# Spectral mixing and a top-80 expert layer: the kept rows chosen from short lists made during the forward part

## The chip, the cores and the metric

The kernel runs on one core of a Trainium2 chip. The metric is the device time of one execution in microseconds. The kernel before takes 773.69 us (median of three runs, 771.19 to 774.16). Every time below comes from one profiled execution of the kernel before.

## The reference

Two steps in fp32. First a spectral filter over each of 8 sequences of 2496 rows of 256 numbers:

```python
X = np.fft.rfft(x, axis=1)               # x: (8, 2496, 256)
Y = X * (filt_r + 1j * filt_i)[None]     # 1249 frequencies x 256
y = np.fft.irfft(Y, n=2496, axis=1)      # (8, 2496, 256) -> 19968 rows
```

Then an expert layer on the 19968 rows of `y`. A row belongs to the one expert of 8 with its largest logit; of each expert's rows the 80 with the largest gate weight are kept, all other rows of the output are zero:

```python
logits = x @ w_gate                      # (19968, 8)
expert_idx = np.argmax(logits, axis=1)
gate_w = softmax(logits)[arange, expert_idx]
for e in range(8):
    tok_idx = rows of expert e, cut to the 80 largest gate_w
    h = np.maximum(x[tok_idx] @ w1[e], 0.0)               # 256 -> 1024
    out[tok_idx] = gate_w[tok_idx, None] * (h @ w2[e])    # 1024 -> 256
```

So only 640 of the 19968 rows of `y` are needed as rows; of the others only the logits are.

## The kernel before

A sequence is a grid of 39 x 64 rows, and its transform is two sets of matmuls with a turn between them.

*Start (L155 to L171, L204 to L215, L173 to L181).* `load_tables` puts the tables and the two filters (four pieces of up to 0.66 MB, `fst`) on the DMA queue of ScalarE (ACT). `load_x` brings a sequence's rows in chunks on SyncE's queue (SP). `stage1` multiplies a chunk by `wf_t`, ACT copies the result out of PSUM and stores it to the scratch `d1` in DRAM. `turn_filter` transposes the filters on TensorE.

*Forward part (`manual_schedule`, the loop over sequences at its end).* Here the written order is the order of each engine. For sequence `b` there are twelve steps `u`: `stage2` (matmuls with `d_t`, products with the filter on VectorE, two additions on GpSimd), `stage1` of the sequence after, two steps later `turn`, which stores the spectrum to the scratch `yf[b]` on GpSimd's queue, and `load_t2` for the next sequence. The gate logits of a pair of sequences are worked out from their spectra, in five parts (`logits`), inside the sequences after the pair, and land in `lg`: 128 partitions x 256 rows x 8 experts. The logits of the last pair follow the loop.

*Selection (`select`, L532 to L858).* It starts when all of `lg` is there. Softmax and argmax give each row a key per expert (its gate weight under its own expert, else zero); keys are transposed to 128 partitions of 1248. The 80th largest key of each expert is searched for in 9 rounds of 7 counting passes over all keys (L667), with a small matmul behind each round. Then positions are worked out by running sums, and one-hot matmuls turn them into lists (L766 to L781): `idxb` (up to 128 kept rows of each sequence), and for each of the 80 places of an expert `idxs` (output row), `idxg` (place in `y_sel`) and `gate`. `more` counts rows beyond 128 of a sequence.

*Zero stores and weights.* `zero_t` is stored 32 times over `out`, 0.64 MB each, on the SP queue, and the weights of the first five experts are loaded on that queue (two transfers of 1.05 MB for an expert).

*Back transform (`back`).* For each sequence: an indirect DMA on GpSimd's queue gathers 128 rows (10 KB each) of a table of inverse-transform rows by `idxb`, SP loads the spectrum `yb` (2.62 MB), TensorE makes 20 transposes of the gathered rows and 20 matmuls with `yb`, and the 128 rows go to the scratch `y_sel`. `gt`, `yb` and the rest have two buffers each. If `more` is above zero, further lists of rows follow, else the branch is skipped. At the branch the SP queue waits until its transfers have landed.

*Expert stage (`gather`, `layer1`, `layer2`).* Per expert: gather 80 rows of `y_sel` by `idxg`, two layers of matmuls, scatter to `out` by `idxs`.

Outside `manual_schedule` the framework chooses the order of the instructions of each engine from their dependences; a tile pool that opens where another has closed waits for the last use of the memory under it.

## Time and profile before

| | us |
|---|---|
| median of three runs | 773.69 |
| the profiled execution, its own time | 774.0 |
| its span in the trace | 772.2 |
| PE busy | 482.4 (62%) |
| VectorE (DVE) busy | 362.8 (47%) |
| GpSimd (POOL) busy | 226.8 (29%) |
| ScalarE (ACT) busy | 123.4 (16%) |

Busy time is summed over the whole span, and stages with different limits lie in it: a share says little until the span is cut into stages. PE is TensorE's matmuls, PEld its weight loads, which run beside them. The transfers of the whole span are 162.15 MB, 210 GB/s on the mean. The granted clock (PEclk) is TensorE's, as a fraction of full speed, 1.00 being 2.4 GHz and 0.50 being 1.2 GHz. The DMA share is the mean busy share of the core's 16 DMA engines.

### The profile page before, as it was taken

To read this page: it belongs to the slowest core of one execution; us is meant where nothing else is said; L and a number is where in the kernel's file an instruction comes from. 1 tells how busy PE (TensorE), PEld (TensorE's weight loads), DVE (VectorE), ACT (ScalarE), POOL (GpSimd) and SP (SyncE) were. 2 spreads that over 40 slices of the span, in tenths; PEclk is the share of its full clock that TensorE was granted. 3 is DMA by queue.
4 is the path that set the end of the run, shared out by engine and by line. 5 is a ranking of instruction groups with operands and counts; after the bars stand their busy time and mean duration, and the time that the engine had idled before them with its cause. 6 is when DMAs were issued, how large, how long until landed. Compare 5 with 4: busy or idle time off the path is not lost. (4 is left out here: it accounts for less than half of the span.)

```text
span 772.2 us, 8200 instructions
## 1 busy us (share of the span) xinstructions
PE 482.4 (62%) x3004; PEld 387.4 (50%) x3004; DVE 362.8 (47%) x519; ACT 123.4 (16%) x210; POOL 226.8 (29%) x302
## 2 busy tenths in 40 slices
PE   3258797998899979892100000122431999987996
PEld 1146666775777768780100000102431888877885
DVE  1033343253435434637798999899980221210110
ACT  0213342333333424220000000000000100100111
POOL 1003645354636555763510000001931000002111
PEclk9567998999999999985555555555555999995999
DMA  9999999799989997999992000000007789812720
GB/s 175 234 285 219 295 314 304 225 276 310 301 267 293 314 304 251 297 415 408 366 382 71 0 0 0 0 0 1 0 1 312 274 334 374 346 50 76 235 73 14
DMA packets 63573, 162.15 MB, mean 210 GB/s; under 512 B 6519, under 2 KB 38263, under 8 KB 61159
## 3 DMA queue, kind: packets, MB, share of 16 engines
q1 hardware_dynamic: 47222, 101.84, 41.0%
q10 hardware_dynamic: 8624, 26.94, 11.8%
q0 software_dynamic: 7680, 32.77, 11.5%
q8 instruction: 26, 0.43, 0.2%
q14 instruction: 21, 0.16, 0.1%
HBM read 96.26 MB, written 65.27 MB: 209 GB/s over the span
## 5 line engine op out<-in xcount | busy, mean ns | idle before, releaser
L241 DVE TENSOR_TENSOR p<-pb,ft 128x512 f32<-128x512 f32 x160 | 102.7, 686 | 156.0 <-issue 91.6
L212 PE MATMUL pa<-x,wf_t 117*120 117x512 f32 x176 | 94.5, 663 | 30.4 <-ACT t L214 17.5
L246 POOL TENSOR_TENSOR yt<-p,p 128x256 f32<-128x256 f32 x80 | 57.9, 724 | 170.5 <-DVE p L241 170.2
L234 PE MATMUL pb<-d_t,t 128*128 128x128 f32 x640 | 88.2, 283 | 22.1 <-DMA t<-d 22.1
L667 DVE TENSOR_SCALAR_CACHE_REDUCE junk<-keyT,thr 128x1248 bf16<-128x1248 f32 x63 | 95.3, 1512 | 6.5 <-ACT keyT L636 4.2
L234 PEld LDWEIGHTS pb<-d_t,t 128*128 128x128 f32 x640 | 81.8, 198 | 32.6 <-issue 32.5
L258 PEld LDWEIGHTS py<-gi,yt 128*128 128x128 f32 x640 | 82.9, 192 | 28.3 <-issue 14.2
L258 PE MATMUL py<-gi,yt 128*128 128x136 f32 x640 | 90.1, 284 | 10.6 <-POOL yt L248 9.9
L768 POOL TENSOR_TENSOR vals<-vv,oh_bf 128x1536 bf16<-128x1536 bf16 x8 | 34.8, 4382 | 148.5 <-PE psl L780 148.4
L403 PE MATMUL pr<-yb,wt 128*128 128x256 f32 x320 | 71.7, 379 | 0.0
L672 PE MATMUL pc<-cnt,grp 128*128 128x7 f32 x18 | 5.3, 365 | 105.1 <-DVE junk L667 105.1
L214 ACT COPY t<-pa 120x512 f32<-120x512 f32 x88 | 51.3, 586 | 114.2 <-PE pa L212 104.7
L403 PEld LDWEIGHTS pr<-yb,wt 128*128 128x128 f32 x320 | 59.6, 190 | 7.4
L266 ACT COPY ysp<-py 128x544 f32<-128x544 f32 x80 | 48.9, 612 | 87.8 <-PE py L258 82.2
L212 PEld LDWEIGHTS pa<-x,wf_t 117*120 117x120 f32 x176 | 32.0, 202 | 59.0 <-issue 39.4
L248 POOL TENSOR_TENSOR yt<-p,p 128x256 f32<-128x256 f32 x80 | 57.8, 722 | 0.0
L672 PEld LDWEIGHTS pc<-cnt,grp 128*128 128x128 f32 x18 | 4.5, 312 | 106.1 <-DVE junk L667 70.6
L400 ACT COPY wt<-pw 128x512 f32<-128x512 f32 x16 | 9.4, 587 | 291.8 <-PE pw L398 291.8
L780 PE MATMUL psl<-vals,ohp 128*80 128x48 bf16 x256 | 18.6, 242 | 38.2 <-DVE ohp L775 38.2
L780 PEld LDWEIGHTS <-ohp 128*80 128x80 bf16 x256 | 17.7, 181 | 40.6 <-DVE ohp L775 40.6
L775 DVE TENSOR_TENSOR ohp<-pos,iota_bf 128x2560 bf16<-128x2560 bf16 x8 | 37.4, 4738 | 0.0
L464 PEld LDWEIGHTS ph<-xs,w 128*128 128x128 f32 x256 | 36.1, 227 | 0.6
(161 smaller groups left out, 482.6 us busy)
## 6 DMA issues: line engine op xcount, KB each, us to landing
t<-d SPq DMA_DIRECT2D x80, 256.0 KB
yf<-ysp POOLq DMA_DIRECT2D x40, 512.0 KB, 7.5
yb<-yf SPq DMA_DIRECT2D x8, 2560.0 KB
out_dram<-zero_t SPq DMA_DIRECT2D x32, 624.0 KB
d<-t ACTq DMA_DIRECT2D x40, 480.0 KB
x<-in_x_dram SPq DMA_DIRECT2D x120, 156.0 KB
w<-in_moe_w_dram SPq DMA_DIRECT2D x16, 1024.0 KB
d<-t ACTq DMA_DIRECT2D x8, 240.0 KB
```

The costliest lines, as they stand in the source:

```text
L212: nc.tensor.matmul(out=ps[0:NM1], lhsT=wf_t, rhs=xt[:, 2 * i:2 * i + 2, :], start=True, stop=True)
L214: nc.scalar.copy(out=t1[:, 2 * i:2 * i + 2, :], in_=ps[0:NM1])
L234: nc.tensor.matmul(out=ps[:, i, cb], rhs=d_t[:, s, :], start=True, stop=True, lhsT=st["t2", b, s // SG][:, s % SG, 128 * cb:128 * cb + 128])
L241: nc.vector.tensor_tensor(out=pt, in0=ps[:].rearrange("p s c r q -> p (s c) r q"), in1=f.unsqueeze(2).to_broadcast([128, 2 * NDB, 2, NQ]), ...
L246: nc.gpsimd.tensor_tensor(out=yt[:, :, 0, :], in0=pr[0][:, :, 0, :], in1=pr[1][:, :, 1, :], op=AL.subtract)
L248: nc.gpsimd.tensor_tensor(out=yt[:, :, 1, :], in0=pr[0][:, :, 1, :], in1=pr[1][:, :, 0, :], op=AL.add)
L258: nc.tensor.matmul(out=ps[:, i, 136 * cb:136 * cb + 136], rhs=gi[:, cb, :], lhsT=yt[:, 2 * i + cb].rearrange("p r q -> p (r q)"), start=Tr ...
L266: nc.scalar.copy(out=ys[:, m:m + 2, :], in_=ps[:, :, 0:ZW])
L403: nc.tensor.matmul(po[:], lhsT=wt[:, s, :], rhs=yb[:, s, :], start=(start and s == 0), stop=(stop and s == NS - 1))
L667: nc.vector.tensor_scalar(out=junk[:], in0=keys, scalar1=thr[:, j:j + 1], scalar2=None, op0=AL.is_ge, op1=AL.add, accum_out=cnt[:, j:j + 1],)
L775: nc.vector.tensor_tensor(out=ohp[:], in0=pos[:, t0:t0 + TC].unsqueeze(2).to_broadcast([PG, TC, cap]), in1=iota_bf[:].unsqueeze(1).to_broa ...
L780: nc.tensor.matmul(psl[0:cap, :], lhsT=ohp[:, t, :], rhs=vals[:, t, :, :], start=(t0 + t == 0), stop=(t0 + t == T - 1))
```

## The change

*Gating in the forward part.* When a pair's logits are done, `gating` works in six parts: softmax and argmax of this pair alone, the gates stored to a scratch `gates_dram` (four stores on GpSimd's queue), keys transposed on TensorE, and VectorE's `max` and `max_index` on each sequence. A transposed partition is 8 experts x 16 groups of rows, so for each sequence there are 128 *cells* of 156 keys, and the 8 largest of each cell with their places go to `cand` and `code`. Pairs 0 to 2 are gated in sequences 3, 5 and 7 (steps 1, 2, 4, 5, 7, 9), the last pair behind the loop.

*`pick` in place of `select`.* Of each partition's 64 candidates the 16 largest are taken, brought to one partition per expert by a matmul (256 numbers), and ten times `max`, nine times `match_replace` give the 80 largest and so the edge. Counts, positions and the lists come from small matmuls and one-hot products on the kept candidates. `gate` is gathered from `gates_dram` by eight indirect DMAs (`gather_gates`).

*Fallback.* `bad` is above zero if a cell's eighth candidate is kept, a partition keeps 16 or more, a sequence keeps more than 128 rows, or an expert's count isn't 80. Only then do the old `select`, the back transform and the spill lists run, inside one `If`.

*Start.* Filters come in ten pieces through the buffers of `t2` on GpSimd's queue, as do `d_t`, `gi`, `e_t` and `wi_t`.

*SP queue.* Two spectra are asked for ahead of `pick`; the zero stores and the weights are spread over the rounds of the back transform.

The diff, cut (the constants, most of `pick` and the one-hot lists are left out; a line that is only "..." marks each cut):

```diff
-                for k, filt in enumerate((filt_r, filt_i)):
-                    for q in range(2):
-                        off, step = (0, C) if q == 0 else (N1 * C, -C)
-                        nc.scalar.dma_start(
-                            out=fst[k][32 * q:32 * q + 32],
-                            in_=bass.AP(tensor=filt.tensor, offset=filt.offset + off,
-                                        ap=[[N1 * C, 32], [step, NS], [1, C]]))
-                nc.scalar.dma_start(out=d_t, in_=d_dram.ap())
...
+                nc.gpsimd.dma_start(out=d_t, in_=d_dram.ap())
...
+        def load_filter(k, g):
+            fst[k, g] = t2pool.tile([128, SG, C], F32, name=f"fst_{k}_{g}", tag="t2")
+            filt = (filt_r, filt_i)[k]
+            for q in range(2):
+                off, step = (0, C) if q == 0 else (N1 * C, -C)
+                nc.gpsimd.dma_start(
+                    out=fst[k, g][32 * q:32 * q + 32],
+                    in_=bass.AP(tensor=filt.tensor, offset=filt.offset + off + step * SG * g,
+                                ap=[[N1 * C, 32], [step, SG], [1, C]]))
...
+        def gating(b2, part):
+            T2 = 2 * NJ
+            l = lg[:, T2 * b2:T2 * b2 + T2, :]
...
+            if part == 0:
+                mx = row("mx")
+                nc.vector.tensor_reduce(out=mx[:], in_=l, axis=AX.X, op=AL.max)
+                st["sh"] = big("sh")
+                nc.vector.tensor_tensor(out=st["sh"][:], in0=l, in1=bc(mx[:]), op=AL.subtract)
+                st["ex"] = big("ex")
+                nc.scalar.activation(out=st["ex"][:], in_=st["sh"][:], func=AF.Exp)
+            elif part == 1:
+                st["first"] = big("first")
+                nc.vector.scalar_tensor_tensor(
+                    out=st["first"][:], in0=st["sh"][:], scalar=0.0,
+                    in1=rev[:].unsqueeze(1).to_broadcast([128, T2, E]),
+                    op0=AL.is_equal, op1=AL.mult)
+                st["fm"] = row("fm")
+                nc.vector.tensor_reduce(out=st["fm"][:], in_=st["first"][:], axis=AX.X,
+                                        op=AL.max)
+            elif part == 2:
+                gw = row("gw")
+                nc.vector.tensor_reduce(out=gw[:], in_=st["ex"][:], axis=AX.X, op=AL.add)
+                nc.vector.tensor_scalar(out=gw[:], in0=gw[:], scalar1=1e-9, scalar2=None,
+                                        op0=AL.add)
+                st["gw"] = row("gwr")
+                nc.vector.reciprocal(out=st["gw"][:], in_=gw[:])
+            elif part == 3:
+                oh = big("oh")
+                nc.vector.tensor_tensor(out=oh[:], in0=st["first"][:], in1=bc(st["fm"][:]),
+                                        op=AL.is_equal)
+                st["key"] = big("key")
+                nc.vector.tensor_tensor(out=st["key"][:], in0=oh[:], in1=bc(st["gw"][:]),
+                                        op=AL.mult)
+                for h in range(2):
+                    for i in range(2):
+                        g0 = (2 * b2 + i) * S + NJ * h
+                        nc.gpsimd.dma_start(
+                            out=bass.AP(tensor=gates_dram.tensor, offset=gates_dram.offset + g0,
+                                        ap=[[N2, N1], [1, NJ]]),
+                            in_=st["gw"][64 * h:64 * h + N1, NJ * i:NJ * i + NJ])
+            elif part == 4:
+                pk = fps.tile([128, 4, 2, 64], F32, name=f"pk_{b2}", tag="f")
+                for i in range(4):
+                    nc.tensor.transpose(pk[:, i].rearrange("p h n -> p (h n)"),
+                                        st["key"][:, 16 * i:16 * i + 16, :], ident[:])
+                st["kt"] = gpool.tile([128, 2, N1, 2, 2], F32, name=f"kt_{b2}", tag="kt")
+                for i in range(2):
+                    nc.scalar.copy(out=st["kt"][:, i].rearrange("p n h c -> p c h n"),
+                                   in_=pk[:, 2 * i:2 * i + 2, :, 0:N1])
+            else:
+                for i in range(2):
+                    b = 2 * b2 + i
+                    k = st["kt"][:, i].rearrange("p n h c -> p (n h c)")
+                    nc.vector.max(out=cand[:, b, :], in_=k)
+                    nc.vector.max_index(out=cidx[:, b, :], in_max=cand[:, b, :], in_values=k)
+                nc.vector.scalar_tensor_tensor(
+                    out=code[:, 2 * b2:2 * b2 + 2, :], in0=cidx[:, 2 * b2:2 * b2 + 2, :],
+                    scalar=16.0, in1=cbase[:, 2 * b2:2 * b2 + 2, :], op0=AL.mult, op1=AL.add)
...
+            for k, g in kg[:7]:
+                load_filter(k, g)
             load_tables(1)
...
+                    if b % 2 == 1 and b > 1 and u in (1, 2, 4, 5, 7, 9):
+                        gating(b // 2 - 1, (1, 2, 4, 5, 7, 9).index(u))
...
+            for part in range(NG):
+                gating(B // 2 - 1, part)
...
-    for i in range(4 * B):
-        nc.sync.dma_start(
-            out=out[i * ZR:i * ZR + ZR, :].rearrange("r d -> (r d)").rearrange(
-                "(p m) -> p m", p=128),
-            in_=zero_t[:])
-    for e in range(3):
-        load_weights(e)
+    zeros = list(range(4 * B))
+    def put_zeros(n):
+        for i in zeros[:n]:
+            nc.sync.dma_start(
+                out=out[i * ZR:i * ZR + ZR, :].rearrange("r d -> (r d)").rearrange(
+                    "(p m) -> p m", p=128),
+                in_=zero_t[:])
+        del zeros[:n]
...
+        for i in range(NTOP):
+            src = pall if i == 0 else left
+            nc.vector.max(out=top[:, 8 * i:8 * i + 8], in_=src[:])
+            if i + 1 < NTOP:
+                nc.vector.match_replace(out=left[:], in_to_replace=top[:, 8 * i:8 * i + 8],
+                                        in_values=src[:], imm_value=-1.0)
...
+        viol = sp.tile([128, 4], F32, name="viol")
+        nc.vector.tensor_reduce(out=viol[:, 0:1], in_=kept[:, :, KC - 1], axis=AX.X, op=AL.add)
+        nc.vector.tensor_scalar(out=viol[:, 1:2], in0=rcnt[:], scalar1=float(KR), scalar2=None,
+                                op0=AL.is_ge)
+        vb = sp.tile([128, B], F32, name="vb")
+        nc.vector.tensor_scalar(out=vb[:], in0=poff[:, 1, 0:B], scalar1=128.0, scalar2=None,
+                                op0=AL.is_gt, op1=AL.add, accum_out=viol[:, 2:3])
+        vt = sp.tile([128, 1], F32, name="vt")
+        nc.vector.tensor_scalar(out=vt[:], in0=tau[:], scalar1=1e-20, scalar2=None, op0=AL.is_gt)
+        nc.vector.scalar_tensor_tensor(
+            out=viol[:, 3:4], in0=poff[:, 2, 1:2], scalar=float(cap), in1=vt[:],
+            op0=AL.not_equal, op1=AL.mult)
...
+    def gather_gates():
+        nc.gpsimd.memset(gate[:], 0.0)
+        for e in range(E):
+            nc.gpsimd.indirect_dma_start(
+                out=gate[:, e:e + 1], out_offset=None, in_=gates_dram[:, :],
+                in_offset=bass.IndirectOffsetOnAxis(ap=idxs[:, e:e + 1], axis=0),
+                bounds_check=N - 1, oob_is_err=False)
...
+        yb = {b: spectrum(mp, b, f"{b}") for b in range(2)}
+        put_zeros(8)
+        with (
+            tc.tile_pool(name="pick", bufs=1) as sp,
+            tc.tile_pool(name="pkps", bufs=1, space=PSUM) as pp,
+        ):
+            pick(sp, pp)
         for b in range(B):
-            back(mp, mps, f"{b}", lambda: spectrum(mp, b, f"{b}"), 128 * b, idxb[:, b:b + 1])
...
+            back(mp, mps, f"{b}", lambda: yb.pop(b), 128 * b, idxb[:, b:b + 1])
+            if b + 2 < B:
+                yb[b + 2] = spectrum(mp, b + 2, f"{b + 2}")
+            put_zeros(3)
+            if b >= 3:
+                load_weights(b - 3)
+            if b == 2:
+                gather_gates()
...
+    n_bad = nc.values_load(bad[0:1, 0:1], min_val=0, max_val=1 << 20)
+    with tc.If(n_bad > 0):
+        select(tc, lg, cap, ident, ident_bf, iota, iota_i, pid, pid_i, lane, idxs, idxg, gate,
+               idxb, more, nof, ohb)
+        with (
+            tc.tile_pool(name="xp2", bufs=1) as mp,
+            tc.tile_pool(name="xps2", bufs=1, space=PSUM) as mps,
+        ):
+            for b in range(B):
+                back(mp, mps, f"g{b}", lambda: spectrum(mp, b, f"g{b}"), 128 * b,
+                     idxb[:, b:b + 1])
+            for t in range(NX):
+                ix = spill_lists(tc, mp, mps, t, cap, nof, ohb, iota, idxg)
+                po = None
+                for b in range(B):
+                    po = back(mp, mps, f"x{t}_{b}", lambda: spectrum(mp, b, f"x{t}_{b}"),
+                              128 * (B + t) if b == B - 1 else None, ix[:, b:b + 1],
+                              start=(b == 0), stop=(b == B - 1), acc=po, pad=True)
...
-    for e in range(3, 5):
-        load_weights(e)
```

On SP, between the last loads of the forward part and the spectrum of round 3 of the back transform. `w_0` to `w_4` are experts' weights, `yb` spectra, `y_sel` the rows made by a round (`yr`) or the zeros behind them. Before (the 32 zero stores and `w_0` to the first half of `w_2` stand ahead of this):

```order
L358 DMA w_2_2775<-in_moe_w_dram 128x8x256
L425 DMA y_sel<-zero_t 128x256 x4
L356 DMA w_3_6100<-in_moe_w_dram 128x2x1024
L358 DMA w_3_6102<-in_moe_w_dram 128x8x256
L356 DMA w_4_6104<-in_moe_w_dram 128x2x1024
L358 DMA w_4_6106<-in_moe_w_dram 128x8x256
L426 TENSOR_LOAD more
L426 ISA x2
L413 DMA yb_3491<-yf_81 128x5120
L413 DMA yb_3550<-yf_82 128x5120
```

and after:

```order
L496 DMA out_dram<-zero_t 128x1248 x10
L713 DMA yb_2954<-yf_119 128x5120
L713 DMA yb_2956<-yf_120 128x5120
L496 DMA out_dram<-zero_t 128x1248 x10
L488 DMA w_0_3387<-in_moe_w_dram 128x2x1024
L708 DMA y_sel<-yr_3168 128x256
L713 DMA yb_3171<-yf_121 128x5120
L490 DMA w_0_3389<-in_moe_w_dram 128x8x256
L708 DMA y_sel<-yr_3230 128x256
L713 DMA yb_3233<-yf_122 128x5120
L496 DMA out_dram<-zero_t 128x1248
```

The spectra have moved ahead of 22 zero stores and all weights, and a spectrum no longer has only spectra and small stores around it. The memory under `yb_2954` and `yb_2956` is that of the last gating, so they, and all that stands behind them, wait for its end.

On SP, at the end of the back transform. Before:

```order
L413 DMA yb_3904<-yf_88 128x5120
L408 DMA y_sel<-yr_3840 128x256
L408 DMA y_sel<-yr_3899 128x256
L408 DMA y_sel<-yr_3958 128x256
L427 COMPARE_AND_BRANCH
```

and after:

```order
L496 DMA out_dram<-zero_t 128x1248 x3
L488 DMA w_3_3583<-in_moe_w_dram 128x2x1024
L490 DMA w_3_3585<-in_moe_w_dram 128x8x256
L708 DMA y_sel<-yr_3641 128x256
L496 DMA out_dram<-zero_t 128x1248 x3
L488 DMA w_4_3647<-in_moe_w_dram 128x2x1024
L490 DMA w_4_3649<-in_moe_w_dram 128x8x256
L738 DMA y_sel<-zero_t 128x256 x4
L739 TENSOR_LOAD bad
L739 ISA x2
L740 COMPARE_AND_BRANCH
```

Before, three small stores stand in front of the branch at which the queue waits for its transfers; after, the last rounds' zero stores and weights stand there too.

On ACT, at the start of the program. `fst` are the filters, `t` the results of `stage1`, `d` the scratch. Before:

```order
L155 DMA wf_t<-wf_tbl 117x120
L160 DMA fst_131<-in_filt_r_dram 32x5120
L160 DMA fst_131<-in_filt_r_dram 32x20x256
L160 DMA fst_132<-in_filt_i_dram 32x5120
L160 DMA fst_132<-in_filt_i_dram 32x20x256
L164 DMA d_t<-d_tbl 128x2560
L165 DMA gi<-in_moe_w_gate_dram 128x8
L166 DMA gi<-in_moe_w_gate_dram 128x8
L214 ACT_TABLE_LOAD
L214 COPY t_0_0_166<-pa_0_0_167 120x512
```

and after:

```order
L205 DMA wf_t<-wf_tbl 117x120
L267 ACT_TABLE_LOAD
L267 COPY t_0_0_219<-pa_0_0_220 120x512
L267 COPY t_0_0_219<-pa_0_1_223 120x512
L268 DMA d_0_218<-t_0_0_219 120x1024
```

The seven transfers that stood ahead of ACT's first copy are gone from its queue.

## Rows read from the trace of the kernel before

**Rows 1.** Stages: from:to, length, busy (instructions) PE PEld DVE ACT POOL, PEclk, DMA share, GB/s.

```profile
0.00:59.90 59.90, 22.65 (x103) 12.60 (x103) 8.88 (x14) 7.53 (x12) 3.44 (x12) 0.71 0.95 231
59.90:320.00 260.10, 235.51 (x1487) 184.43 (x1488) 105.28 (x160) 89.17 (x150) 132.69 (x211) 0.96 0.93 282
320.00:339.30 19.30, 17.17 (x144) 16.45 (x143) 11.64 (x19) 4.90 (x8) 17.66 (x28) 1.00 1.04 387
339.30:355.20 15.90, 12.39 (x63) 7.70 (x62) 4.87 (x6) 1.55 (x3) 2.97 (x9) 0.60 1.02 413
355.20:598.60 243.40, 37.66 (x332) 31.71 (x333) 205.56 (x274) 3.59 (x5) 49.68 (x21) 0.50 0.29 109
598.60:692.90 94.30, 91.00 (x480) 78.03 (x480) 19.99 (x32) 9.39 (x16) 5.63 (x6) 0.98 0.72 280
...
697.00:772.20 75.20, 66.02 (x400) 56.45 (x400) 6.53 (x16) 7.27 (x16) 14.66 (x16) 0.84 0.31 102
```

**Rows 2.** Groups: line, engine, operation, out<-in, count | busy, mean ns | idle before.

```profile
L667 DVE TENSOR_SCALAR_CACHE_REDUCE junk<-keyT,thr 128x1248 bf16<-128x1248 f32 x63 | 95.3, 1512 | 6.5 <-ACT keyT L636 4.2
...
L273 POOL DMA_DIRECT2D yf<-ysp x40 | 31.0, 776 | 0.0
...
L605 DVE TENSOR_REDUCE mx<-lg 128x256 f32<-128x2048 f32 x1 | 2.3, 2275 | 0.0
...
L840 DVE TENSOR_TENSOR ohl<-plcf,iota 80x1024 f32<-80x1024 f32 x1 | 1.2, 1221 | 0.0
L351 POOL MEMSET zero_t<- 128x1248 f32 x1 | 1.1, 1138 | 2.4 <-PE pa L212 2.4
...
L683 DVE TENSOR_SCALAR tau<-base 128x1 f32<-128x1 f32 x1 | 0.2, 155 | 0.0
```

**Rows 3.** Timeline from 353 us: start, duration, engine, line, operation [idle before <-releaser].

```profile
353.04 2.17 DVE L308 COPY lg<-pl 39x512 f32<-39x512 f32 x2 [3.75 <-PE pl L303]
...
355.38 2.91 DVE L566 TENSOR_SCALAR n_i<-pid_i 128x1 int32<-128x1 int32 x1
...
356.19 2.02 POOL L690 MEMSET wT<- 128x2048 bf16 x1
```

**Rows 4.** Timeline, end of the selection and first round of the back transform.

```profile
582.44 0.17 DVE L847 CAST idxb<-plist 128x8 int32<-128x8 f32 x1 [3.68 <-PE plist L845]
582.54 1.24 SPq L413 DMA_DIRECT2D yb<-yf  x2
583.51 1.07 POOL L389 DMA_INDIRECT gt<-rows_tbl,idxb  x1 [16.95 <-DVE idxb L847]
...
598.62 1.73 PE L398 MATMUL pw<-ident,gt 128*128 128x128 f32 x7 [16.21 <-DMA gt<-rows_tbl,idxb]
...
611.43 0.32 SPq L413 DMA_DIRECT2D yb<-yf  x1
```

**Rows 5.** The tile `gt` (gathered table rows), time from issue to landing.

```profile
DMA to landing us min/median/max: 6.6/10.2/19.8
```

**Rows 6.** Timeline, end of the back transform.

```profile
692.42 0.42 DVE L407 COPY yr<-pr 128x256 f32<-128x256 f32 x1 [7.51 <-PE pr L403]
...
696.97 0.94 POOL L447 DMA_INDIRECT xg<-y_sel,idxg  x1 [34.74 <-DVEq L427]
```

**Rows 7.** Two stretches in which the DMA engines are full, columns as in Rows 1.

```profile
340.00:403.00 63.00, 15.90 (x75) 10.77 (x74) 47.07 (x69) 4.65 (x8) 21.29 (x21) 0.52 1.03 388
583.00:599.00 16.00, 0.38 (x2) 0.41 (x3) 0.00 (x0) 0.00 (x0) 2.04 (x2) 0.50 0.98 392
```

**Rows 8.** Timeline of the start.

```profile
12.26 11.23 ACTq L160 DMA_DIRECT2D fst<-in_filt_i_dram  x2
...
32.91 1.07 ACT L214 COPY t<-pa 120x512 f32<-120x512 f32 x2
33.55 8.86 PE L212 MATMUL pa<-x,wf_t 117*120 117x512 f32 x14 [17.46 <-ACT t L214]
...
59.86 2.05 PE L234 MATMUL pb<-d_t,t 128*128 128x128 f32 x8 [9.35 <-DMA t<-d]
```

More of the change, by code (lines that the diff above doesn't have):

```diff
@@ new lines @@
+    same = consts.tile([128, 128], BF16, name="same")
+    nc.vector.tensor_scalar(out=same[:], in0=ecol[:], scalar1=lane[:, 0:1], scalar2=None,
+                            op0=AL.is_equal)
+    before = consts.tile([128, 128], BF16, name="before")
+    nc.vector.tensor_scalar(out=before[:], in0=iota[:], scalar1=pid[:, 0:1], scalar2=None,
+                            op0=AL.is_gt)
+    before_e = consts.tile([128, 128], BF16, name="before_e")
+    nc.vector.tensor_tensor(out=before_e[:], in0=before[:], in1=same[:], op=AL.mult)
@@ L124 @@
+    ones_bf = consts.tile([128, 128], BF16, name="ones_bf")
+    nc.gpsimd.memset(ones_bf[:], 1.0)
     yf = [dpool.tile([128, NS, C], F32, name=f"yf_{b}") for b in range(B)]
@@ L150 @@
         ft = [tpool.tile([128, NS, NDB, NQ], F32, name=f"ft{i}") for i in range(2)]
-        fst = [stg.tile([NQ, NS, C], F32, name=f"fst{i}") for i in range(2)]
+        fst = {}
         def load_tables(part):
@@ L317 @@
                 load_x(0, ch)
+            kg = [(k, g) for k in range(2) for g in range(NS // SG)]
+            for k, g in kg[:7]:
+                load_filter(k, g)
             load_tables(1)
```

213 lines of the change are left out of this document (183 added, 30 removed).

## Prediction

> **What bounds the kernel now.** I read the busy table by stage first. In [rows 1] the reader is to see seven stretches of one execution (span 772.2 us; its own time 774.0 us, the median of the three runs 773.69, so the sum below is made against 774.0 and needs no correction). From 59.9 to 320 us TensorE is busy 235.5 of 260.1 us: the forward part is a TensorE stage with transfers close behind (DMA share 0.93). From 320 to 339.3 it is GpSimd that is full, 17.66 of 19.3 us. From 355.2 to 598.6 us, 243.4 us, TensorE does 37.7 us of work, the DMA share is 0.29, and VectorE is busy 205.6 us: this is the selection, and the granted clock is 0.50 in it. From 598.6 to 692.9 TensorE is full again (91.0 of 94.3 us), in the per-sequence back transform. The expert stage takes the last 75.2 us.
>
> The groups by line name the work of the selection: 63 counting passes of 1512 ns (95.3 us) lead [rows 2]. The timeline gives its ends. The logits of the last pair of sequences are copied by VectorE until 355.2 us [rows 3]; the row lists `idxb` are written at 582.44 us; the first gather is issued 1 us later and lands when TensorE starts, 598.6 us [rows 4]. At the end of the back transform, 4.1 us lie between the last copy at 692.9 and the gather that opens the expert stage [rows 6].
>
> **The change part by part.** For the price of a small VectorE instruction I take a line through [rows 2, 6]: 256 elements 0.42 us, 1024 elements 1.22, 2048 elements 2.28, so about 0.15 us plus 1.04 ns per element.
>
> *Selection, removed: 243.4 us* [rows 1], from the last logits to TensorE's first transpose. In its place stand three pieces in a row.
> (a) Gating of the last pair. Seven passes over 512 elements at 0.68 us (4.8), reciprocal and offset (0.7, the reciprocal has no row of that size), four transposes with two copies behind them (about 2), the list instructions (about 1.2) and the hops between engines: 10 us. The other three pairs are gated inside the forward part.
> (b) `pick`. Nineteen instructions of MAX and MATCH_REPLACE over 256 elements have no row in this trace. The nearest is a pass of 256 elements at 0.42 us [rows 6]; the bounds are 0.15 us (a one-element instruction) and 1.51 us (the slowest list-like pass here, the counting pass) [rows 2]. At 0.42 they cost 8.0 us, and lie between 2.9 and 28.7. The rest: two one-hot passes of 1024 elements (2.4), one of 1280 (1.5), four passes of 128 to 256 (1.3), six list instructions of 64 elements (1.3), some 24 tiny ones at 0.16 (3.8), three or four trips over TensorE at about 0.75 and the small matmuls (4). Together 22 us, bounds 17 and 43.
> (c) The first gather. Its eight kind landed after 6.6 to 19.8 us, median 10.2 [rows 5]. The first of before took 15.1 us because two 2.6 MB spectra were issued in the same microsecond [rows 4]; now those were issued 22 us earlier, and zero stores share the engines. I take 10.2.
> Sum: 10 + 22 + 10.2 = 42.2 us for 243.4, that is -201.2.
>
> *What the selection covered.* In the long stretch the SP queue put out most of the 32 zero stores and five experts' weights, for nothing. That cover is gone. The order of the SP queue now has ten zero stores, then the first two spectra, which wait for the end of the last gating (the memory under them is its lists), ten more zero stores, and the other twelve and the weights between the spectra of the back transform. Call the end of the last gating T0. After T0 and before the expert stage there are 8 spectra of 2.62 MB, 22 zero stores of 0.64, 10 weight halves of 1.05, 8 gathers of 1.31 and 1.6 MB of small ones (sizes from the code): 21.0 + 14.1 + 10.5 + 10.5 + 1.6 = 57.6 MB. With the engines full the trace moves 388 to 392 GB/s [rows 7]: 147 us. TensorE's own path from T0 is 22 + 10.2 + 94.3 = 126.5 us, so the transfers are the longer of the two. Spectra still come in time: in one round of 11.6 us (94.3 / 8) 4.5 MB can move, a spectrum and a gather are 3.9, and what exceeds it stands behind the spectrum in the queue. So TensorE keeps its 94.3 us, and the excess piles up at the end. There the SP queue waits for every transfer before the gathers of the expert stage go out, as before, but before the queue was empty. About 6 us of idle engines come on top: two spectra, ten zero stores and a weight half behind them, and two gathers, 15.3 MB, are done 39 us after T0, and the next spectrum is issued only after the first round, at 22 + 10.2 + 12.8 = 45 (12.8 from the first transpose to the next spectrum's issue, [rows 4]). I allow 2 us from the last landing to the gather: T0 + 155, where the old layout would give 126.5 + 4.1 = 130.6: +24.4 us. A gain on (b) or (c) is mostly given back here, and so is a loss.
>
> *Start.* Filters and tables leave the ACT queue for POOL's. Before, ACT could not copy until 32.9 us because its queue still held filter transfers, and TensorE idled 17.5 us for it; the first spectral matmul came at 59.86 [rows 8]. ACT is free at once now, but the engines were at a share of 0.95 in these 59.9 us [rows 1], so most of the 17.5 us turns into a wait for bytes. What must be there before 59.86 is nearly the same, about 11.5 MB; only `e_t` can come later. I take -6 us, with -14 (nearly the 17.5) and +3 (the filter pieces delay the x loads) as ends.
>
> *Forward part.* Gating of three pairs adds some 6 us of VectorE, 1 us of TensorE and four small stores on GpSimd for each. In the sequences with stage 1 these lie under TensorE. In the last sequence GpSimd is full, so its four stores (about 0.78 us each, by the issue of a GpSimd transfer) and the zero fill (1.1 us), now queued between its additions, are paid [rows 2]: with the TensorE share, +5 us, ends 0 and 12.
> A rule of the Trainium skill speaks against this term. [Rows 3] show a VectorE instruction on one element that takes 2.91 us and ends when GpSimd's 2.02 us fill ends, at 358.2. The Trainium skill, SBUF — State Buffer, section "SBUF: two separate sides", says that VectorE and GpSimd share one pair of ports, and that the one which has it keeps it for its whole instruction; the trace agrees at this place (2.91 us). By that rule the seven gating passes of the pair gated there could not run beside a full GpSimd, some 5 us more: 601 instead of 596, an estimate.
>
> *Expert stage*: same instructions, 75.2 us.
>
> **Sum:** 774.0 - 201.2 + 24.4 - 6 + 5 = 596.2. I predict 596 us.
>
> **The rivals.**
> 1. *The drain is hidden.* The tail stays at 4.1 us if the engines move clearly more than 392 GB/s when zero stores (into DRAM) and spectra (out of it) run together, or the queue never idles. For it: a share of 0.72 in the back transform leaves room [rows 1]. Against: the count of bytes. Time 596 - 24 = 572.
> 2. *Transfers are slower when mixed.* In the forward part a share of 0.93 moved only 282 GB/s [rows 1], 303 at a full share. At that rate 57.6 MB take 190 us, 43 more: the spectra then come late and the back transform itself stretches. Against: those are pieces of 1 to 4 KB, these mostly 4 KB and more. Time 639.
> 3. *The list instructions are slow,* 1.51 us each: 21 us more in `pick`, of which the tail gives a part back, since its transfers go on meanwhile. About 18 stay: 614.
> 4. *Slower than before: the fallback runs.* `bad` is above zero if a cell's eighth entry is kept, a row keeps 16, a sequence more than 128, or an expert's count is not 80. Then, after 594, come the old selection (227.4 us from the last logits to `idxb`, [rows 3, 4]), eight rounds of back transform with their first gather (692.9 - 582.6 = 110 us), and four spill lists of eight rounds, 32 times 11.6 at the least (371): about 1300 us. The point is one integer. From the reference's own inputs I count at most 4 kept in a cell (8 would fail), 11 in a row (16), 90 in a sequence (128), and at every expert's edge the 80th and 81st gate differ by 24 or more units in the last place. Only an inexact copy of a gate through TensorE could raise it, and it would in every run.
>
> **How the numbers follow.** Forecast 0.70, with a range of its own of 578 to 615: the ends of start (-8, +9) and forward part (-5, +7), the rate from 370 to 413 GB/s (about -7, +9), added as independent. Rival 1: 0.12; rival 2: 0.09; rival 3: 0.05; rival 4: 0.04. The range reaches down past rival 1 and up past rival 3, short of most of rival 2 and all of 4: 565 to 622. A measurement of this kernel tells a change from none at about 0.5%, 4 us. Every case but the fourth is faster by far more: faster 0.95, slower 0.04, 0.01 for the rest.
>
> **What would show it.** The page of the changed kernel should have no counting passes; MAX and MATCH_REPLACE near 0.4 us; 30 to 50 us from the last logits to the first transpose of gathered rows; rounds of the back transform still near 11.6 us; and then 20 to 30 us in which no engine computes while the DMA share is near 1. Stage 2 should start near 54 us. I am wrong if spectra hold up TensorE between rounds, if the gap before the expert stage is as short as before, if the forward part grows by more than 12 us, or if lines of `select` appear at all.

## The result

The changed kernel takes 594.98 us (median of four runs, 594.03 to 602.84) against 772.44 for the kernel before in the same sessions, a ratio of 0.7727 with a 95% interval of 0.7668 to 0.7786. The prediction was 596. The profiled execution is the longest of the four (602.84, span 600.7); where that matters the profiles of the experiments, which share most of the code, stand beside it. Medians in this text are over all executions of a version, while the ratios leave out two executions that were over 1.5% above the fastest of their version (one of weights late, one of bulk on ACT).

The stages of the changed kernel, columns as in [rows 1]: forward part, gating of the last pair, lists, first gather, first round, the other seven rounds, the gap, expert stage.

```profile
52.90:359.25 306.35, 271.88 (x1702) 213.71 (x1702) 145.04 (x232) 99.42 (x170) 161.81 (x253) 0.93 0.85 271
359.25:368.16 8.91, 1.08 (x4) 0.71 (x4) 6.83 (x17) 1.34 (x3) 2.07 (x4) 0.50 0.02 6
368.16:391.24 23.08, 3.64 (x41) 2.59 (x41) 18.99 (x77) 0.00 (x0) 2.57 (x5) 0.50 0.96 372
391.24:402.21 10.97, 0.00 (x0) 0.00 (x0) 0.00 (x0) 0.00 (x0) 6.85 (x7) 0.50 1.03 422
402.21:416.70 14.49, 14.48 (x66) 12.61 (x67) 2.50 (x4) 1.17 (x2) 3.83 (x4) 0.80 0.64 236
416.70:502.00 85.30, 79.70 (x416) 67.84 (x414) 17.48 (x29) 8.20 (x14) 4.73 (x5) 0.98 1.00 401
502.00:523.03 21.03, 0.00 (x0) 0.00 (x0) 0.01 (x1) 0.00 (x0) 0.00 (x0) 0.54 0.87 328
...
523.03:600.70 77.67, 66.30 (x400) 56.56 (x400) 6.53 (x16) 7.25 (x16) 14.72 (x16) 0.83 0.31 99
```

The 243.4 us of the selection in [rows 1] have become 8.9 + 23.1 + 11.0 = 43.0. In the gap of 21.0 us, where 4.1 stood [rows 6], no engine computes and the DMA share is 0.87. From the end of the last gating to the first expert gather (523.03 - 368.16) it is 154.9 us.

The groups of the list instructions, columns as in [rows 2]:

```profile
L537 DVE MAX8 top<-left 8x8 f32<-8x256 f32 x9 | 3.7, 416 | 0.3
L539 DVE MATCH_REPLACE8 left<-top,left 8x256 f32<-8x256 f32 x8 | 3.2, 397 | 0.0
...
L431 DVE FIND_INDEX8 cidx<-cand,kt 128x8 uint32<-128x156 f32 x8 | 2.5, 314 | 0.0
L430 DVE MAX8 cand<-kt 128x8 f32<-128x156 f32 x8 | 2.5, 310 | 1.7 <-ACT kt L424 1.7
```

MAX over 256 numbers takes 0.416 us, a plain pass over 256 took 0.42 [rows 6]. Each MATCH_REPLACE has a short value load ahead of it (0.08), so one step of the chain is 0.9 us.

The timeline of the last rounds (start, duration, engine, line, operation, idle before):

```profile
475.49 1.28 SPq L713 DMA_DIRECT2D yb<-yf  x1
476.82 1.94 SPq L496 DMA_DIRECT2D out_dram<-zero_t  x3
...
478.95 0.70 PE L703 MATMUL pr<-yb,wt 128*128 128x256 f32 x2 [2.00 <-DMA yb<-yf]
...
490.01 0.42 DVE L707 COPY yr<-pr 128x256 f32<-128x256 f32 x1 [9.03 <-PE pr L703]
...
501.59 0.42 DVE L707 COPY yr<-pr 128x256 f32<-128x256 f32 x1 [7.51 <-PE pr L703]
...
508.75 7.47 SPq L738 DMA_DIRECT2D y_sel<-zero_t  x4
523.03 0.92 POOL L765 DMA_INDIRECT xg<-y_sel,idxg  x1 [55.44 <-SPq L740]
```

The seventh round waits 2.0 us for its spectrum and takes 15.4 us (474.6 to 490.0) where its neighbours take 11.6. The first expert gather waits for the SP queue at the branch.

### The profile page after: what moved, and what is told of

It reads as the page before. It is cut to its first block, busy times and chain, and to the rows that moved or that the text cites. A ratio compares the mean times of both kernels' runs of the same rounds, so it can differ in the third digit from the quotient of the medians.

```text
span 600.7 us, 7565 instructions
## 1 busy us (share of the span) xinstructions
PE 459.4 (76%) x2729; PEld 365.2 (61%) x2729; DVE 208.4 (35%) x406; ACT 125.1 (21%) x217; POOL 213.9 (36%) x332
## 3 DMA queue, kind: packets, MB, share of 16 engines
q0 software_dynamic: 9792, 38.12, 18.3%
q10 hardware_dynamic: 6610, 21.69, 11.6%
## 5 line engine op out<-in xcount | busy, mean ns | idle before, releaser
L265 PE MATMUL pa<-x,wf_t 117*120 117x512 f32 x176 | 96.6, 675 | 19.5 <-DMA x<-in_x_dram 19.4
L299 POOL TENSOR_TENSOR yt<-p,p 128x256 f32<-128x256 f32 x80 | 59.8, 748 | 128.6 <-DVE p L294 124.8
L311 PE MATMUL py<-gi,yt 128*128 128x136 f32 x640 | 89.8, 283 | 18.5 <-POOL yt L301 18.4
L703 PE MATMUL pr<-yb,wt 128*128 128x256 f32 x320 | 74.2, 388 | 2.4 <-DMA yb<-yf 2.4
L301 POOL TENSOR_TENSOR yt<-p,p 128x256 f32<-128x256 f32 x80 | 60.6, 757 | 0.0
L765 POOL DMA_INDIRECT xg<-y_sel,idxg x8 | 7.3, 911 | 84.6 <-SPq L740 55.4
L698 PE MATMUL pw<-ident,gt 128*128 128x128 f32 x160 | 24.5, 297 | 15.2 <-DMA gt<-rows_tbl,idxb 12.5
L782 PE MATMUL ph<-xs,w 128*128 128x80 f32 x256 | 36.1, 311 | 0.0
L698 PEld LDWEIGHTS pw<-ident,gt 128*128 128x128 f32 x160 | 19.6, 151 | 20.2 <-DMA gt<-rows_tbl,idxb 12.5
L796 PE MATMUL po<-w,hT 128*80 128x256 f32 x128 | 31.5, 396 | 0.0
L326 POOL DMA_DIRECT2D yf<-ysp x40 | 30.6, 765 | 1.2 <-issue 1.2
L689 POOL DMA_INDIRECT gt<-rows_tbl,idxb x8 | 7.7, 963 | 61.6 <-PE pw L698 47.6
## 6 DMA issues: line engine op xcount, KB each, us to landing
x<-in_x_dram SPq DMA_DIRECT2D x120, 156.0 KB
```

The source lines that it names most:

```text
L265: nc.tensor.matmul(out=ps[0:NM1], lhsT=wf_t, rhs=xt[:, 2 * i:2 * i + 2, :], start=True, stop=True)
L299: nc.gpsimd.tensor_tensor(out=yt[:, :, 0, :], in0=pr[0][:, :, 0, :], in1=pr[1][:, :, 1, :], op=AL.subtract)
L301: nc.gpsimd.tensor_tensor(out=yt[:, :, 1, :], in0=pr[0][:, :, 1, :], in1=pr[1][:, :, 0, :], op=AL.add)
L311: nc.tensor.matmul(out=ps[:, i, 136 * cb:136 * cb + 136], rhs=gi[:, cb, :], lhsT=yt[:, 2 * i + cb].rearrange("p r q -> p (r q)"), start=Tr ...
L698: nc.tensor.transpose(ps[:, i, :], gt[:, 128 * s:128 * s + 128], ident[:])
L703: nc.tensor.matmul(po[:], lhsT=wt[:, s, :], rhs=yb[:, s, :], start=(start and s == 0), stop=(stop and s == NS - 1))
```

## The experiments

All are edits of the changed kernel. Two theories stood against each other for the end of the back transform. *Bytes*: from the last gating (T0) to the first expert gather, the engines have a fixed number of bytes to move, and the list step and TensorE's rounds lie beside them. *Fixed gap*: the 21 us are a wait of the queue itself and follow TensorE's path whatever is moved. The table has each run's median with its ratio to the kernel before, and from its profile the length from T0 to the first expert gather, the mean rate in it, their product, and the gap behind the last round.

| run | us | ratio (95%) | T0 to gather | GB/s | MB | gap |
|---|---|---|---|---|---|---|
| changed kernel | 595.0 | 0.7727 (0.7668 to 0.7786) | 154.9 | 373 | 57.8 | 21.0 |
| chain twice | 600.2 | 0.7776 (0.7730 to 0.7821) | 159.2 | 363 | 57.8 | 17.3 |
| weights late | 590.3 | 0.7613 (0.7561 to 0.7665) | 146.2 | 359 | 52.5 | 12.6 |
| zeros first | 593.3 | 0.7671 (0.7611 to 0.7731) | 156.8 | 351 | 55.0 | 10.7 |
| old SP order | 600.9 | 0.7763 (0.7726 to 0.7800) | 163.6 | 337 | 55.1 | 4.2 |
| start on ACT | 595.4 | 0.7728 (0.7676 to 0.7779) | 155.6 | 371 | 57.7 | 20.6 |
| gating at the end | 599.3 | 0.7773 (0.7723 to 0.7823) | 137.0 | 359 | 49.2 | 4.9 |
| gates on ACT | 595.6 | 0.7728 (0.7678 to 0.7778) | 155.7 | 371 | 57.8 | 20.8 |
| full queue | 593.8 | 0.7684 (0.7654 to 0.7714) | 156.0 | 352 | 54.9 | 6.6 |
| full queue, late weights | 591.1 | 0.7641 (0.7604 to 0.7678) | 150.9 | 325 | 49.0 | 4.9 |
| bulk on ACT | 598.1 | 0.7728 (0.7675 to 0.7781) | 161.4 | 313 | 50.5 | 4.2 |
| bulk on ACT, early | 586.6 | 0.7599 (0.7567 to 0.7630) | 147.8 | 342 | 50.5 | 4.2 |

**Chain twice.**

```diff
-        for i in range(NTOP):
+        for i in [i for _ in range(2) for i in range(NTOP)]:
```

> The chain of ten MAX and nine MATCH_REPLACE that finds the 80 largest stands twice in the list step (the second pass repeats the first; the lists are unchanged). The chain took 9.1 us in the profile of the changed kernel. Theory 1 (the end of the back transform is set by the bytes that the engines still have to move after the last gating): the first gather comes about 9 us later, the gap before the expert stage shrinks from 21 us to about 12, and the time stays within 2 us of 595. Theory 2 (the gap has a fixed cause, the wait of the queue at the branch or the issue of its last transfers, and the list step is on the path): the gap stays near 21 us and the time is 604.

Measured: the lists took 9.2 us longer (32.28 in the second row below, from 23.08), the way from T0 to the first expert gather 4.3 longer, the gap 3.8 shorter, and the median rose by 5 (the intervals of the two ratios overlap). So about half was given back, which is between the two theories. The bytes are the same. In the first round the SP queue stands at that round's small store with little behind it in flight, and the rate there is lower than in the changed kernel (189 GB/s, from 236): a longer list step lengthens the time in which the queue has nothing to give. The edit moved more than the chain: the framework also put half a weight and two more zero stores (2.3 MB) ahead of that store.

```profile
348.36:357.28 8.92, 1.09 (x4) 0.72 (x4) 6.84 (x17) 1.34 (x3) 2.07 (x4) 0.50 0.52 201
357.28:389.56 32.28, 3.64 (x41) 2.59 (x41) 27.25 (x105) 0.00 (x0) 2.58 (x5) 0.50 0.96 378
...
400.03:413.80 13.77, 13.77 (x66) 12.03 (x67) 2.50 (x4) 1.17 (x2) 3.83 (x4) 0.84 0.52 189
```

**Weights late.**

```diff
-            if b >= 3:
+            if b in (3, 4):
                 load_weights(b - 3)
...
     gather(1)
+    for e in range(2, 5):
+        load_weights(e)
```

> The weights of experts 2, 3 and 4 are asked for after the first two gathers of the expert stage, five of the six transfers behind the branch: 5.2 MB fewer must land before the gathers. Theory 1 (bytes): 5.2 MB at 0.39 MB per us is 13 us less, the gap falls to 8 us or less, time about 582, and the expert stage is no longer than before since its share of the engines is 0.31. Theory 2 (fixed gap): 595. Theory 3 (the weights then come late in the expert stage): the gap falls but the expert stage grows by as much, 595.

The way to the gather fell by 8.7 us, not 13, and the expert stage grew from 77.7 to 82.7. Fixed gap falls; the third theory holds for a part.

**Zeros first.**

```diff
-        yb = {b: spectrum(mp, b, f"{b}") for b in range(2)}
-        put_zeros(8)
+        put_zeros(18)
+        yb = {b: spectrum(mp, b, f"{b}") for b in range(2)}
```

> Eighteen zero stores instead of ten stand ahead of the first two spectra on the SP queue, so that the engines, idle at a share of 0.02 for the 8.9 us of the last gating, have work there. The bytes are the same. Theory 1 (bytes): 8.9 us at 0.39 is 3.4 MB fewer after the last gating, the gap falls from 21 to about 12 us, time about 587. Theory 2 (fixed gap): 595. Theory 3 (the first two spectra come late behind the stores and the first round waits for them): the first round starts or stretches by up to 8 us, 595 or a little more.

The engines were full during the last gating (share 1.02, from 0.02), 2.8 MB fewer were left, and the way from T0 to the first expert gather grew by 1.9 us. The median is near the 595 of the fixed gap, but the gap itself fell by half. Its stages from the first gather on show why, and before them the first list instruction.

```profile
363.30 0.23 DVE L521 MAX8 row<-cand 128x8 f32<-128x64 f32 x1 [3.43 <-DMA gates<-gwr]
...
386.29:393.29 7.00, 0.01 (x1) 0.01 (x1) 0.00 (x0) 0.00 (x0) 5.47 (x6) 0.50 0.73 260
393.29:406.60 13.31, 13.31 (x66) 11.70 (x67) 2.49 (x4) 1.17 (x2) 5.23 (x6) 0.87 0.47 161
406.60:506.00 99.40, 86.36 (x416) 71.96 (x414) 17.41 (x29) 8.21 (x14) 4.74 (x5) 0.91 1.01 398
506.00:516.65 10.65, 0.00 (x0) 0.00 (x0) 0.00 (x0) 0.00 (x0) 0.00 (x1) 0.66 0.65 185
```

With the engines full, the stores of the gates land late: VectorE waits 3.4 us for them, and the lists take 26.4 us instead of 23.1. (So do the later runs with more zero stores ahead of the spectra, by 3.3 to 4.7 us; in the changed kernel there is no such wait.) For 20 us the share is 0.73 and 0.47: only three stores stood behind the spectra on SP before the first round's small store. What was left then filled the rounds, TensorE waited three times for spectra that came behind it (9.4 us in all), and seven rounds took 99.4 us instead of 85.3.

**Old SP order.**

```diff
+        put_zeros(32)
+        for e in range(3):
+            load_weights(e)
         yb = {b: spectrum(mp, b, f"{b}") for b in range(2)}
-        put_zeros(8)
...
-            put_zeros(3)
-            if b >= 3:
-                load_weights(b - 3)
...
+    for e in range(3, 5):
+        load_weights(e)
     gather(0)
```

> The SP queue as in the kernel before: all 32 zero stores and the weights of three experts ahead of the first spectrum, the other weights behind; selection by short lists as in the changed kernel. Theory 1 (bytes): 26.7 MB ahead of the first spectra keep the engines full from 339 us to about 408, the first two spectra land at about 420, the first round waits some 15 to 20 us for them, the rest of the back transform is undisturbed and the gap is 4 to 8 us: the sum moves by -5 to +3, 590 to 598. Theory 2 (what matters is when the spectra come): the late first round is paid in full and the gap stays, 610 or more.

600.9, just above the first theory's range and far from the second's. TensorE waited 13.2 us for the first spectrum, the first round ended 41 us after its first transpose, and the gap fell to 4.2: the gap is there only where transfers are left. The framework changed TensorE's order here too: the transposes of the first two rounds and eight of the third (411.39) stand ahead of the first round's matmuls (426.54). They were done before the wait of 13.2 us began, so the order did not delay that round.

**Start on ACT.**

```diff
-                nc.gpsimd.dma_start(out=d_t, in_=d_dram.ap())
+                nc.scalar.dma_start(out=d_t, in_=d_dram.ap())
```

(and so for the filter pieces, `gi`, `e_t` and `wi_t`)

> The start's tables and filter pieces are issued on ACT's queue instead of GpSimd's, all else as in the changed kernel. In the profiles the first spectral matmul came at 59.86 us before and at 52.95 after. Theory 1 (ACT's queue held up its copies): the first spectral matmul comes at 58 to 61 us and the time is 5 to 8 us longer, about 601. Theory 2 (the earlier start is due to the pieces and the order of bytes, not to the queue): it stays at 53, time 595.

The time stayed, and the first spectral matmul came no later.

```profile
26.15 1.07 ACT L267 COPY t<-pa 120x512 f32<-120x512 f32 x2
26.78 7.97 PE L265 MATMUL pa<-x,wf_t 117*120 117x512 f32 x14 [14.08 <-ACT t L267]
...
51.69 1.62 PE L287 MATMUL pb<-d_t,t 128*128 128x128 f32 x6 [2.10 <-DMA t<-d]
```

TensorE again waits 14 us for ACT's copies, and stage 2 starts at 51.7. The queue is not what brought the start forward. What else of that edit did (the smaller pieces, or that three of ten come later) was not tried.

**Gating at the end.**

```diff
-                    if b % 2 == 1 and b > 1 and u in (1, 2, 4, 5, 7, 9):
-                        gating(b // 2 - 1, (1, 2, 4, 5, 7, 9).index(u))
...
-            for part in range(NG):
-                gating(B // 2 - 1, part)
+            for b2 in range(B // 2):
+                for part in range(NG):
+                    gating(b2, part)
```

> The gating of pairs 0 to 2 is taken out of the forward part and stands behind the last logits, with that of pair 3. From the first spectral matmul to the last logits the kernel before took 295.3 us and the profiled execution of the changed kernel 306.3. Theory 1 (gating inside the forward part costs it about 8 us, by waits of TensorE for GpSimd's additions): that stretch falls to 295 to 299, the three gatings cost about 7 us each behind it, and the time is about 595 - 8 + 21 = 608. Theory 2 (the gating is hidden there and the 11 us are variation of the transfers from run to run): the stretch stays at 300 or more and the time is about 616.

599.3, better than either. The forward part took 293.2 us; in the eleven profiles with gating inside it took 293.7 to 306.3, median 296.9. So the gating costs it about 4 us by these medians, though with one profile against a spread of 12.6 us this is no more than an estimate, and the 306.3 of the changed kernel's profile are mostly that execution's own. The three gatings cost 26.5 us behind the logits, and 17.9 came back: during them twenty zero stores and a weight went out, only 49.2 MB were left, and the gap fell to 4.9.

**Gates on ACT.**

```diff
-                        nc.gpsimd.dma_start(
+                        nc.scalar.dma_start(
                             out=bass.AP(tensor=gates_dram.tensor, ...
```

> The sixteen stores of the gates are issued on ACT's queue instead of GpSimd's. A group of four took 2.07 us of GpSimd in the profile. Theory 1 (the stores stand between GpSimd's additions, for which TensorE waits): the waits of TensorE for the additions fall from 18.4 us by about 5, the forward part is 4 to 6 us shorter, time about 590. Theory 2 (they are hidden): within 2 us of 595.

TensorE's waits for GpSimd's additions fell from 18.4 us to 13.1, as the first theory has it (in the nine other profiles with these stores on GpSimd's queue and gating inside they are 16.3 to 18.3), but its forward part took 299.0 us and the time did not move: the second theory.

**Fallback.** The count that decides the branch is raised by one.

```diff
-        nc.vector.tensor_copy(out=bad[:], in_=misc[0:1, 49:50])
+        nc.vector.tensor_scalar(out=bad[:], in0=misc[0:1, 49:50], scalar1=1.0, scalar2=None,
+                                op0=AL.add)
```

> The count that decides the branch is raised by one, so the fallback always runs: the old selection, the back transform again and four rounds of further lists. By the rows of the kernel before this is 227 us + 110 us + 32 times 11.6 us at the least behind a start at about 517: about 1300 us. If the fallback were cheap (lists of rows that are empty cost little, since their gathers move nothing), 940 to 1000.

1673.16 us in its one run. The forty gathers of the fallback are issued some 20 us apart, not 11.6: its pool has one buffer of each tile, so that a round's gather waits for the round before.

**Full queue.**

```diff
+        put_zeros(18)
         yb = {b: spectrum(mp, b, f"{b}") for b in range(2)}
-        put_zeros(8)
+        put_zeros(14)
+        load_weights(0)
...
-            put_zeros(3)
```

(the weights of experts 1 to 4 in the rounds)

> All 32 zero stores and one expert's weights are ahead of the first round's small store on the SP queue: 18 zero stores, two spectra, 14 zero stores, expert 0's weights, then the rounds with the other weights between them. In the eighteen-first run the queue held only three zero stores behind the spectra and the engines' share fell to 0.73 and 0.47 until the first round's rows were stored. Theory 1 (the end is set by the bytes left plus the time in which the SP queue stands at a round's small store with nothing behind it in flight): no such hole, some 54 MB at 0.39 after the last gating, 139 to 143 us from there to the first expert gather instead of 155, time about 582. Theory 2 (the bytes ahead of a spectrum delay it by as much as they save later): the third spectrum is late, the rounds stretch, 592 to 596.

The hole was filled: 417 GB/s in the first round, from 236. But the third round ended 27.6 us after the second. TensorE's timeline there:

```profile
426.11 0.66 PE L698 MATMUL pw<-ident,gt 128*128 128x128 f32 x4 [0.35 <-DVE wt L700]
428.27 1.06 PE L698 MATMUL pw<-ident,gt 128*128 128x128 f32 x8 [1.51 <-DMA gt<-rows_tbl,idxb]
...
438.39 1.94 PE L698 MATMUL pw<-ident,gt 128*128 128x128 f32 x8 [6.56 <-DMA gt<-rows_tbl,idxb]
440.12 12.22 PE L703 MATMUL pr<-yb,wt 128*128 128x256 f32 x46
```

After the third round's transposes (to 426.8) come those of the fourth (428.27) and the first eight of the fifth (438.39), and only then the third's matmuls: with the bulk moved, the framework has put TensorE's instructions in another order, and the fifth round's gather, landing at 438.4, holds the third. The loss has theory 2's size, but in this round not its mechanism: the DMA packets of the third spectrum end at about 427 us, 13 us before its matmuls begin. A late spectrum comes later, in the seventh round, and costs 2.7 us. The full queue itself was thus not tried under the old order of TensorE.

**Full queue, late weights.** As above, with the weights of experts 1 and 2 in the rounds and those of 3 and 4 behind the gather (one element of it is copied into the tile first):

```diff
+    for e in range(3, 5):
+        load_weights(e, after=xgs[0])
```

> As the run with the full queue, and the weights of experts 3 and 4 are asked for only when the first expert gather has landed (a one-element copy into their tiles orders them): 4.2 MB fewer before it. Theory 1: 50 MB at 0.39 is 128 us, less than TensorE's path of 23 + 11 + 95 + 4 = 133, so the path sets the end: 133 to 138 us from the last gating to the first expert gather, a gap of 4 to 6 us, the expert stage at 77 to 79 us, time about 577. Theory 2 (the spectra are late): rounds stretch, 585 or more. Theory 3 (late weights stretch the expert stage): 5 us of it come back, 582.

591.1, with the same order on TensorE (the third round ends 27.4 us after the second) and no loss in the expert stage (76.8 us).

**Bulk on ACT.** Fourteen zero stores on ACT's queue, held back until T0 by a one-element write of GpSimd; weights of experts 1 and 2 tied to rounds 1 and 3.

```diff
+        nc.gpsimd.tensor_scalar(out=zero_t[0:1, 0:1], in0=code[0:1, B - 1, 0:1], scalar1=0.0,
+                                scalar2=None, op0=AL.mult)
+        put_zeros(14, nc.scalar)
```

> Eighteen zero stores ahead of the first two spectra on the SP queue as before; the other fourteen go out on ACT's queue right behind the last gating, so that no spectrum stands behind a zero store; expert 0's weights follow the first two spectra on SP, those of experts 1 and 2 are tied to the rows of rounds 1 and 3, and those of experts 3 and 4 to the first expert gather. Theory (the end is set by bytes, and by a spectrum that stands behind bulk in its own queue): 50 MB after the last gating are 128 us, below TensorE's path of about 133; with two queues the third spectrum is at most 5 us late; 133 to 142 us from the last gating to the first expert gather, a gap of 4 to 7 us, and the time is 576 to 584. Rival (two queues share the engines no better, the third spectrum is as late as in the run with the full queue, 14 us): 590. Rival (the SP queue's own waits set the end): a gap above 10 us.

598.1, a miss of the edit: that write stood on GpSimd behind the list step, and ACT's issue held its copies. Behind that the rounds did not all run undisturbed: the fifth waited 2.6 us for its spectrum and took 17.3 us.

```profile
388.61 30.16 ACTq L500 DMA_DIRECT2D out_dram<-zero_t  x14
419.20 1.08 ACT L706 COPY wt<-pw 128x512 f32<-128x512 f32 x2 [61.05 <-DMA out_dram<-zero_t]
```

**Bulk on ACT, early.** Against the run before, with twenty instead of eighteen zero stores ahead of the spectra:

```diff
-        nc.gpsimd.tensor_scalar(out=zero_t[0:1, 0:1], ...
-        put_zeros(14, nc.scalar)
+        nc.scalar.activation(out=zero_t[0:1, 0:1], in_=code[0:1, B - 1, 0:1], func=AF.Copy,
+                             scale=0.0)
+        put_zeros(12, nc.scalar)
```

> As the run with bulk stores on ACT's queue, in which these stores were issued only at 388.6 us and held ACT until 419, so that a round waited 18.5 us for ACT's copies; once they were out, the rounds ran undisturbed and the gap was 4 us. Here twenty zero stores stand ahead of the spectra and the other twelve go out on ACT's queue as soon as those twenty have landed, near 367 us (a one-element write by ACT itself orders them). Theory (the loss there was ACT's stall, and the rest holds): ACT is free before the first round needs it at about 404, no stall above 5 us, 133 to 142 us from the last gating to the first expert gather, a gap near 4, time 578 to 585. Rival (stores on a second queue delay the first spectra or the first gather by as much): the first round ends 10 us or more later than in the changed kernel, 590 or more.

586.6 us, ratio 0.7599 (0.7567 to 0.7630), the lowest median of all; its interval lies wholly below that of the changed kernel, but overlaps that of weights late (0.7561 to 0.7665). TensorE's order is that of the changed kernel. It missed the foreseen 578 to 585 and the 133 to 142 us from T0: lists 26.3, first gather 12.8, rounds 104.5 and gap 4.2 make 147.8 us. The lists waited for the stores of the gates as above, ACT's issue lasted from 368.0 to 402.9, the first round took 16.3 us, and the fifth waited 4.2 us for its spectrum.

```profile
447.20:454.00 6.80, 2.18 (x15) 1.62 (x13) 1.54 (x5) 1.17 (x2) 0.00 (x0) 0.89 1.03 438
454.00:466.10 12.10, 12.10 (x50) 10.30 (x49) 1.12 (x2) 0.00 (x0) 0.95 (x1) 0.78 0.99 396
```

**The two theories together.** Neither holds alone. The gap is no fixed wait: it goes from 21.0 to 4.2 us with what is left to move. But the way from T0 isn't set by the bytes alone either: with 55 MB it took 156.0 to 163.6 us, longer than the 154.9 with 57.8 MB, because waits for spectra, another order of TensorE or a queue with nothing to give came in.

## Why the prediction was right, step by step

The forecast of 596 lies 1 us from the median, and that closeness is partly luck: the terms below miss by 1 to 3 us each, in both directions. The inner range, too, was mis-added: its ends taken as independent give 584 to 611, not 578 to 615. The measured time lies in both.

*Selection.* Gating of the last pair 10 us forecast, 8.9 measured; lists 22, 23.1; first gather 10.2, 11.0. Taking a MAX at a plain pass of its size, not at 1.51 us, decided this; rival 3 is out.

*The end of the back transform.* The count of bytes, 57.6 MB, was measured as 57.8, and T0 + 155 as T0 + 154.9. Two steps within it were wrong and cancel. "TensorE keeps its 94.3 us" failed: the rounds took 99.8, the first because its transposes and matmuls began at a granted clock of 0.50, the seventh for its late spectrum (2.0 us of wait), which the prediction had named as a sign of being wrong. And the gap is 21.0, not 28.5: where the bytes set the end, what the rounds take longer the gap is shorter. "Mostly given back" was mis-sized: of 9.2 us more in the lists 4.3 stayed. Rival 1 (hidden drain) is out by the gap, rival 2 (303 GB/s when mixed) by 401 GB/s in the rounds.

*Start.* -6 forecast, -6.9 measured, but not for the reason given: with the transfers on ACT's queue the start is as early.

*Forward part.* +5 forecast; +11.0 in this profile, +1.6 by the median of the eleven (296.9, from 295.3). Without the excess of this execution (306.3 - 296.9) its 602.8 would be 593.4, near the other three runs (594.0 to 595.9). The rule on shared ports was weighed there at 5 us more, for all seven long passes. The Trainium skill, SBUF — State Buffer, section "SBUF: two separate sides", ties the lock to VectorE instructions in a two-port mode or with two inputs in SBUF, the latter only against a GpSimd instruction that reads SBUF; four of the seven passes have two inputs. Four instructions of the gating, first beside a busy GpSimd in the last sequence and then alone behind the last logits, and after them one of GpSimd's additions beside the first of these, and one with no gating pass beside it:

```profile
318.50 1.00 DVE L384 TENSOR_TENSOR sh<-lg,mx 128x512 f32<-128x512 f32 x1
325.02 0.80 DVE L399 TENSOR_SCALAR gw<-gw 128x64 f32<-128x64 f32 x1
328.18 1.10 DVE L408 TENSOR_TENSOR key<-oh,gwr 128x512 f32<-128x512 f32 x1
339.14 0.73 DVE L432 SCALAR_TENSOR_TENSOR code<-cidx,cbase 128x16 f32<-128x16 uint32 x1
360.01 0.69 DVE L384 TENSOR_TENSOR sh<-lg,mx 128x512 f32<-128x512 f32 x1
362.77 0.20 DVE L399 TENSOR_SCALAR gw<-gw 128x64 f32<-128x64 f32 x1
364.13 0.69 DVE L408 TENSOR_TENSOR key<-oh,gwr 128x512 f32<-128x512 f32 x1
367.99 0.17 DVE L432 SCALAR_TENSOR_TENSOR code<-cidx,cbase 128x16 f32<-128x16 uint32 x1
...
318.91 1.17 POOL L301 TENSOR_TENSOR yt<-p,p 128x256 f32<-128x256 f32 x1
334.92 0.73 POOL L301 TENSOR_TENSOR yt<-p,p 128x256 f32<-128x256 f32 x1
```

The trace agrees in kind: 0.31 + 0.60 + 0.41 + 0.56 = 1.9 us more for these four on VectorE, while the other long passes of that pair kept their 0.67 to 0.69. GpSimd pays as well: beside each of the four passes with two inputs one addition took 1.02 or 1.17 us instead of 0.73, 1.5 us more for the pair. There are twelve such additions in this profile, four for each pair gated in the forward part, and none in the kernel before or in the run with the gating at the end. Since the whole forward part grew by 1.6 us at the median, the 5 us more of 601 were too many.

*Expert stage.* "Same, 75.2" was 77.7; it is 76.4 to 77.7 in every run whose weights came in time. The cause of these 1 to 2 us was not sought.

*Fallback.* It does not run, as forecast, but its price was mis-sized: 1673, not 1300, since its rounds take 20 us.

## What to carry to other kernels

Before a long stage is cut, count what its queues move under it for nothing: that work does not vanish, and behind the cut it can set the end by its bytes. Placing it elsewhere pays only if nothing that is needed soon stands behind it in the same queue and no queue stands at a small dependent store with nothing else in flight. Two queues, one for what is waited for and one for bulk, gave the lowest median here (586.6). But that run also asked for the last weights late and for more zero stores early, and late weights alone gave 590.3, so what the second queue itself is worth is not shown. Where a framework sets the order, look at what a moved transfer does to the order of the engines too.

## What the runs showed of the hardware

A short wait of TensorE can cost more than itself, by the granted clock. In the changed kernel's seventh round a wait of 2.0 us made 15.4 us of 11.6, with a granted clock of 0.66 in the 5 us behind it. In the last run a wait of 4.2 us made the fifth round 18.9 us (447.2 to 466.1), with a granted clock of 0.78 in the 12.1 us behind it, though TensorE was busy in all of them. It need not be so: in the run with the full queue the seventh round waited 2.7 us, the granted clock stayed at 1.00, and the round took 14.4 us, the wait and little more.
